# Seven block products instead of eight in the first product of a feed-forward block, after clustered attention, in float32

## The chip, the cores and the metric

One core of one Trainium2 chip runs the whole program. The metric is the device time in microseconds (us); the figure of a kernel is the median of several runs. The core has five engines that run side by side, each with its own queue in program order: TensorE multiplies matrices into PSUM (2 KB banks per partition, eight of them), VectorE and ScalarE do elementwise work and can read PSUM, GpSimd does elementwise work on SBUF, and SyncE here only issues transfers. In the profile they are called PE (with PEld for its weight loads), DVE, ACT, POOL and SP.

## The reference

```python
# q, k, v: (4, 8, 768, 64); centroids: (8, 16, 64)
q_assign = argmax(q_n . c_n); k_assign = argmax(k_n . c_n)      # nearest of 16 centroids
mask   = q_assign[:, :, :, None] == k_assign[:, :, None, :]
scores = where(mask, q @ k.T / sqrt(64), -1e9)
attn   = softmax(scores)                                        # denominator + 1e-9
x      = (attn @ v) -> (4 * 768, 8 * 64) = (3072, 512)
# second block: w_in (512, 2048), w_out (2048, 512)
h = x @ w_in
g = h * (1.0 / (1.0 + exp(-1.702 * h)))
out = (g @ w_out).astype(float32)
```

The weights arrive in float64 and are turned into float32 on the chip. A query attends only to keys whose nearest centroid is its own.

## The kernel before

The program walks through 192 units of attention (two heads, 384 queries, 128 keys each), two units in each of 96 turns `t`. A pair of heads is a tile of 128 partitions; four pairs make one batch, and each pair is visited twice, for the first and the second half of its 768 queries. As soon as the four pairs of one half of one batch are normalised, there are four tiles `xT` of 128 features x 384 tokens, and the second block for these 384 tokens is put into a queue `ffn` of 28 steps. The turns that follow take steps from that queue between their attention work. There are 8 such halves. While half `n` is in attention, half `n-1` is in the second block; the last half runs alone at the end.

```python
pairs = ctx.enter_context(tc.tile_pool(name="pairs", bufs=NPB))      # NPB = HP + 1 = 5
wp = ctx.enter_context(tc.tile_pool(name="wp", bufs=3))
gp = ctx.enter_context(tc.tile_pool(name="gp", bufs=NF))             # NF = 16
yp = ctx.enter_context(tc.tile_pool(name="yp", bufs=2))
ps_s = ctx.enter_context(tc.tile_pool(name="ps_s", bufs=2, space=PS))  # two banks each
ps_o = ctx.enter_context(tc.tile_pool(name="ps_o", bufs=1, space=PS))
ps_m = ctx.enter_context(tc.tile_pool(name="ps_m", bufs=3, space=PS))

def bank():                                   # one of three banks, for all but scores and values
    return ps_m.tile([P, 512], FP32, name="m")
# ... (cut)
def first(f):                                 # 128 of the 2048 columns of x @ w_in, transposed
    round_to((f * P // WN + 1) * NCH)
    ps = bank()
    for c in range(NCH):                      # 4 chunks of the 512 features
        nc.tensor.matmul(out=ps[:, 0:HALF], lhsT=w_in[:, c, f * P:(f + 1) * P],
                         rhs=xT[c], start=(c == 0), stop=(c == NCH - 1))
    g = hs[f] = gp.tile([P, HALF], FP32, name="g")
    nc.scalar.activation(out=g, in_=ps[:, 0:HALF], func=AF.Tanh, scale=0.851)
    nc.vector.scalar_tensor_tensor(out=g, in0=g, scalar=1.0, in1=ps[:, 0:HALF],
                                   op0=ALU.add, op1=ALU.mult)

def second(n, part):                          # 4 of 16 chunks of g @ w_out, for 128 tokens
    # ... (cut)
    for f in range(4 * part, 4 * part + 4):
        nc.tensor.matmul(out=ps[:, 0:DM], lhsT=hs[f][:, n * P:(n + 1) * P],
                         rhs=w_out[:, f, :], start=(f == 0), stop=(f == NF - 1))
    if part == NF // 4 - 1:
        y = yp.tile([P, DM], FP32, name="y")
        nc.scalar.mul(y, ps[:, 0:DM], 0.5)
        nc.sync.dma_start(...)

return ([lambda f=f: first(f) for f in range(NF)]
        + [lambda n=n, part=part: second(n, part) for n in range(NH) for part in range(NF // 4)])
```

The order of one turn, shortened:

```python
for t in range(NT + 2):
    # scores of two units (PE), exps (ACT), mask (DVE; for the later batches) and running sums (POOL)
    # values of the two units of the turn before (PE)
    owed = owed + rate if ffn else 0.0        # rate = 28 / 11.5 steps in a turn
    # every third turn: normalise(g): ones x sums (PE), reciprocal 128x384 and product (DVE)
    # prep of a later pair: transposes, nearest centroid (PE, ACT, DVE)
    while owed >= 1 and ffn:
        ffn.popleft()()
        owed -= 1
```

Each fp32 matmul of the program is carried out as two records in the trace, each with a weight load of its own: the 512 matmuls of `first` are 1024 records.

Of the kernel before, what the change touches and what calls it, by code (L numbers as in the profile page):

```python
# [38 lines left out]
def fast(  # L39
# [33 lines left out]
    NF = DF // P  # L73
# [3 lines left out]
    assert D == 64 and NC == 16 and H * NC == P and NJ == 6 and DM == H * D  # L77

    PS = bass.MemoryType.PSUM
    NPB = HP + 1  # L80
    const = ctx.enter_context(tc.tile_pool(name="const", bufs=1))
    inp = ctx.enter_context(tc.tile_pool(name="inp", bufs=3))
    pairs = ctx.enter_context(tc.tile_pool(name="pairs", bufs=NPB))
    wp = ctx.enter_context(tc.tile_pool(name="wp", bufs=3))
# [1 line left out]
    tmp = ctx.enter_context(tc.tile_pool(name="tmp", bufs=3))  # L86
    ap = ctx.enter_context(tc.tile_pool(name="ap", bufs=4))
    xp = ctx.enter_context(tc.tile_pool(name="xp", bufs=HP + 2))
    gp = ctx.enter_context(tc.tile_pool(name="gp", bufs=NF))
    yp = ctx.enter_context(tc.tile_pool(name="yp", bufs=2))  # L90
    dram = ctx.enter_context(tc.tile_pool(
        name="dram", bufs=2, space=bass.MemoryType.DRAM))
    ps_s = ctx.enter_context(tc.tile_pool(name="ps_s", bufs=2, space=PS))
# [124 lines left out]
    hot = const.tile([P, NJ * 4, 32], BF16, name="hot")  # L218
# [12 lines left out]
                            op0=ALU.add)  # L231
# [22 lines left out]
    T, code, qcode, sT, hots = {}, {}, {}, {}, {}  # L254
# [179 lines left out]
    def values(u):  # L434
        g, kt = divmod(u, NJ)
        p, h = split(g)
        if kt == 0:
            o_of[g] = ps_o.tile([P, 512], FP32, name="o")
        A = A_of.pop(u)
        for a in range(2):  # L440
            nc.tensor.matmul(out=o_of[g][a * D:(a + 1) * D, 0:HALF],  # L441
                             lhsT=v_in[p][:, a, kt, :], rhs=A[:, a, :],
                             start=(kt == 0), stop=(kt == NJ - 1))
# [30 lines left out]

    ffn = deque()

    def ffn_chunks(bh):
        b, h = divmod(bh, 2)
        xT = [xT_of.pop(bh * HP + c) for c in range(NCH)]
        hs, ys = {}, {}  # L480

        def first(f):

            round_to((f * P // WN + 1) * NCH)
            ps = bank()
            for c in range(NCH):
                nc.tensor.matmul(out=ps[:, 0:HALF],  # L487
                                 lhsT=w_in[:, c, f * P:(f + 1) * P],
                                 rhs=xT[c], start=(c == 0),
                                 stop=(c == NCH - 1))  # L490
            g = hs[f] = gp.tile([P, HALF], FP32, name="g")
            nc.scalar.activation(out=g, in_=ps[:, 0:HALF], func=AF.Tanh,  # L492
                                 scale=0.851)
            nc.vector.scalar_tensor_tensor(out=g, in0=g, scalar=1.0,  # L494
                                           in1=ps[:, 0:HALF], op0=ALU.add,
                                           op1=ALU.mult)

        def second(n, part):
            round_to(NW // 2 + 4 * (part + 1))
            if part == 0:  # L500
                ys[n] = bank()
            ps = ys[n]
            for f in range(4 * part, 4 * part + 4):
                nc.tensor.matmul(out=ps[:, 0:DM],  # L504
                                 lhsT=hs[f][:, n * P:(n + 1) * P],
                                 rhs=w_out[:, f, :],
                                 start=(f == 0), stop=(f == NF - 1))
            if part == NF // 4 - 1:
                y = yp.tile([P, DM], FP32, name="y")
                nc.scalar.mul(y, ps[:, 0:DM], 0.5)  # L510
                nc.sync.dma_start(
                    out=out[b * S:(b + 1) * S, :].rearrange(
                        "(p j) n -> p j n", j=NJ)[:, h * NH + n, :], in_=y)

        return ([lambda f=f: first(f) for f in range(NF)]
                + [lambda n=n, part=part: second(n, part)
                   for n in range(NH) for part in range(NF // 4)])

# [5 lines left out]
    TB = 2 * HP * TG  # L524

    prep_at = {}
    for p in range(1, NPAIR):
        b, hp = divmod(p, HP)
        for i in range(2 if p == 1 else 0, len(PREP)):
            if p == 1:  # L530
                t = (i - 2) // 2
            elif b == 0:
                t = (hp - 2) * TG + 1 + i // 2
            else:
                t = b * TB + (-20, -8, -2, 1)[hp] + i
            prep_at.setdefault(t, []).append((p, i))
    loads = deque((p, w) for p in range(NPAIR) for w in range(2))
    for _ in range(3):
# [6 lines left out]
        if i in (1, 3) and loads:  # L545
            load_qk(*loads.popleft())

    rate = (NF + NH * (NF // 4)) / (TB / 2 - 0.5)
    owed = 0.0
# [4 lines left out]
    for t in range(NT + 2):  # L554
        us = range(2 * t, 2 * t + 2) if t < NT else ()
        for u in us:
            scores(u)
        if t == 0:
            prep(0, 6)
        for u in us:  # L560
            part(u)
        for u in us:
            exps(u)
        second = t >= TB // 2
        if second:
# [24 lines left out]
        if second and t % 2:  # L590
            round_next()


    ok = const.tile([P, 2, 2 * NPAIR], FP32, name="ok")
# [4 lines left out]
    for _ in range(NF // 2):  # L599
        ffn.popleft()()  # L600
# [5 lines left out]
    nc.vector.tensor_scalar(out=bad, in0=okt, scalar1=-1.0, scalar2=1.0,  # L606
                            op0=ALU.mult, op1=ALU.add)
    while ffn:
        ffn.popleft()()
# [443 lines left out]
```

## Time and profile before

| | |
|---|---|
| median of 3 runs | 1087.48 us (1084.81 to 1087.8) |
| profiled execution, first to last instruction | 1087.3 us |
| granted TensorE clock, mean | 0.990 of full speed |
| PE busy | 1049.0 us (96%), 3982 records |
| DVE busy | 490.8 us (45%) |
| ACT busy | 354.8 us (33%) |
| POOL busy | 296.9 us (27%) |

A row of the list of groups gives the source line, engine and operation, what it writes and reads, partitions x elements, how many there are, then busy time and mean duration of one in ns, and after the second bar the idle time of that engine just before them with what ended most of it. Busy time is the time that is covered: two overlapping matmul records are counted once, so that busy time divided by count is less than the mean duration. In the row of 40 slices a digit is the busy share of a slice in tenths.

### The profile page before, as it was taken

The page shows a single profiled execution, that of the slowest core. Times are in us where ns is not written, and L with a number is a line of the kernel's source. Part 1 is how long each engine was busy: PE and PEld are TensorE (multiplying, and loading weights), DVE is VectorE, ACT ScalarE, POOL GpSimd, SP SyncE. Part 2 cuts the span into 40 slices and gives each one's busy share as a digit, 9 for nine tenths or more (in the row PEclk, how much of TensorE's full clock was granted, in tenths as well). Part 3 has the DMA queues.
Part 4 walks back from the last instruction along what each step waited for, and adds up shares of the span by engine and source line. Part 5 has one row for each costly group of instructions (what it writes and reads, how often), then busy time and mean ns, then how long its engine had stood idle before and what let it go on. Part 6 is the DMA issues. An engine that isn't in the chain of part 4 may idle for free. (4 is left out here: it accounts for less than half of the span.)

```text
span 1087.3 us, 10456 instructions
## 1 busy us (share of the span) xinstructions
PE 1049.0 (96%) x3982; PEld 492.6 (45%) x3982; DVE 490.8 (45%) x744; ACT 354.8 (33%) x665; POOL 296.9 (27%) x168
## 2 busy tenths in 40 slices
PE   7878799999999999999999999999999999999997
PEld 3423344445544455444454445444554445444543
DVE  3889999225442344424453164423552344431200
ACT  3755555223422333223432233223332133311100
POOL 2644223213232333123231142222332333230000
PEclk9998899999999999999999999999999999999999
DMA  7623443110100010002100000010000000000000
GB/s 199 165 81 116 131 133 111 46 49 17 49 23 27 10 30 15 31 25 54 51 23 17 15 20 15 15 48 32 8 7 12 10 10 1 1 10 20 1 11 22
DMA packets 64813, 45.13 MB, mean 42 GB/s; under 512 B 51953, under 2 KB 57585, under 8 KB 64753
## 3 DMA queue, kind: packets, MB, share of 16 engines
q1 hardware_dynamic: 64608, 44.33, 14.3%
q8 instruction: 33, 0.54, 0.2%
q14 instruction: 28, 0.22, 0.1%
q10 hardware_dynamic: 144, 0.03, 0.0%
HBM read 38.04 MB, written 6.31 MB: 41 GB/s over the span
## 5 line engine op out<-in xcount | busy, mean ns | idle before, releaser
L430 POOL TENSOR_TENSOR sum<-sum,A 128x768 f32<-128x768 f32 x128 | 235.5, 1840 | 461.3 <-DVE A L420 364.1
L487 PE MATMUL m<-x,w_in 128*128 128x384 f32 x1024 | 347.1, 494 | 9.7 <-ACT T L267 4.4
L504 PE MATMUL m<-w_out,g 128*128 128x512 f32 x768 | 337.8, 594 | 0.7 <-ACT short L282 0.7
L420 DVE SCALAR_TENSOR_TENSOR A<-qb,code,s 128x384 f32<-128x384 uint8 x288 | 157.6, 609 | 274.6 <-ACT s L409 251.9
L487 PEld LDWEIGHTS m<-x,w_in 128*128 128x128 f32 x1024 | 192.2, 192 | 149.1 <-issue 16.3
L504 PEld LDWEIGHTS m<-w_out,g 128*128 128x128 f32 x768 | 143.3, 190 | 175.6 <-issue 171.5
L494 DVE SCALAR_TENSOR_TENSOR g<-g,m 128x384 f32<-128x384 f32 x128 | 70.0, 553 | 220.4 <-ACT g L492 220.3
L384 PE MATMUL s<-T,T 64*128 64x384 f32 x768 | 152.9, 517 | 9.7 <-ACT A L409 9.6
L409 ACT ACTIVATE s<-s 128x768 f32<-128x768 f32 x144 | 107.9, 792 | 136.0 <-PE s L384 136.0
L441 PE MATMUL o<-A,inv 128*64 128x384 f32 x768 | 146.3, 502 | 0.0
L492 ACT ACTIVATE g<-m 128x384 f32<-128x384 f32 x128 | 61.7, 487 | 196.4 <-PE m L487 196.3
L430 POOL TENSOR_TENSOR sum<-A 128x768 f32<-128x768 f32 x32 | 60.0, 1876 | 215.6 <-DVE A L420 179.5
L384 PEld LDWEIGHTS s<-T,T 64*128 64x128 f32 x768 | 66.6, 189 | 94.6 <-issue 52.2
L456 DVE RECIPROCAL short<-m 128x384 f32<-128x384 f32 x32 | 81.6, 2551 | 25.8 <-PE m L453 25.8
L441 PEld LDWEIGHTS o<-A,inv 128*64 128x64 f32 x768 | 46.8, 137 | 84.8 <-issue 84.1
L510 ACT ACTIVATE y<-m 128x512 f32<-128x512 f32 x24 | 14.3, 595 | 155.8 <-PE m L504 142.7
L468 ACT ACTIVATE short<-short 128x384 f32<-128x384 f32 x32 | 16.7, 523 | 111.2 <-DVE x L458 111.2
L409 ACT ACTIVATE A<-s 128x768 f32<-128x768 f32 x48 | 36.1, 804 | 22.0 <-PE s L398 22.0
L267 ACT COPY T<-m 128x384 f32<-128x384 f32 x64 | 29.7, 480 | 37.2 <-PE m L262 37.1
L262 PE MATMUL m<-ident,in 128*128 128x128 f32 x192 | 33.9, 298 | 3.1 <-ACT T L267 1.7
L163 ACT ACTIVATE e<-e,low 128x512 int32<-128x512 int32 x32 | 23.1, 722 | 28.8 <-DVE e L159 28.8
L262 PEld LDWEIGHTS m<-ident,in 128*128 128x128 f32 x192 | 21.5, 146 | 22.4 <-issue 11.9
(68 smaller groups left out, 373.5 us busy)
## 6 DMA issues: line engine op xcount, KB each, us to landing
raw<-in_moe_w_in_dram SPq DMA_DIRECT2D x16, 512.0 KB
raw<-in_moe_w_out_dram SPq DMA_DIRECT2D x16, 512.0 KB
in<-in_q_dram SPq DMA_DIRECT2D x32, 192.0 KB
in<-in_k_dram SPq DMA_DIRECT2D x32, 192.0 KB
inv<-in_v_dram SPq DMA_DIRECT2D x16, 384.0 KB
out_dram<-y SPq DMA_DIRECT2D x24, 256.0 KB
qb<-line SPq DMA_DIRECT2D x12, 192.0 KB
line<-row SPq DMA_DIRECT2D x12, 1.5 KB
```

What stands on the lines that cost most here:

```text
L262: nc.tensor.transpose(out=ps[:, n * P:(n + 1) * P], in_=qk_in[p, w][:, h * NH + n].rearrange("p a d -> p (a d)"), identity=ident)
L267: nc.scalar.copy(dst, ps[:, 0:HALF])
L384: nc.tensor.matmul(out=ps[:, a, 0:HALF], lhsT=T[p, 1][rows, kt * P:(kt + 1) * P], rhs=T[p, 0][rows, h * HALF:(h + 1) * HALF], start=True, ...
L409: nc.scalar.activation(out=A_of[u] if p < HP else s, in_=s, func=AF.Exp, scale=SCALE)
L420: nc.vector.scalar_tensor_tensor(out=A_of[u][:, a, :], in0=qcode[p][:, a, h * HALF:(h + 1) * HALF], scalar=code[p][:, kt % NH, 1, kt // NH ...
L430: nc.gpsimd.tensor_tensor(out=sum_of[g], in0=A_of[u - 1] if kt == 1 else sum_of[g], in1=A, op=ALU.add)
L441: nc.tensor.matmul(out=o_of[g][a * D:(a + 1) * D, 0:HALF], lhsT=v_in[p][:, a, kt, :], rhs=A[:, a, :], start=(kt == 0), stop=(kt == NJ - 1))
L456: nc.vector.reciprocal(out=rec, in_=ps[:, 0:HALF])
L487: nc.tensor.matmul(out=ps[:, 0:HALF], lhsT=w_in[:, c, f * P:(f + 1) * P], rhs=xT[c], start=(c == 0), stop=(c == NCH - 1))
L492: nc.scalar.activation(out=g, in_=ps[:, 0:HALF], func=AF.Tanh, scale=0.851)
L494: nc.vector.scalar_tensor_tensor(out=g, in0=g, scalar=1.0, in1=ps[:, 0:HALF], op0=ALU.add, op1=ALU.mult)
L504: nc.tensor.matmul(out=ps[:, 0:DM], lhsT=hs[f][:, n * P:(n + 1) * P], rhs=w_out[:, f, :], start=(f == 0), stop=(f == NF - 1))
```

## The change

Write the product of 256 rows of `w_in`-columns, 512 features and 384 tokens as a 2x2x2 product of blocks: the weights' output columns f and f + 8 (row blocks 0 and 1), the features 0..255 and 256..511 (inner blocks), and the tokens 0..191 and 192..383. Eight block products are needed in the plain way. With sums and differences of blocks taken beforehand and others taken afterwards, seven are enough (the scheme of Strassen in Winograd's form). The sums over the weights are taken once; those over `x` once for each half; those over the results for every pair of column blocks. The purpose is to give TensorE one product in eight less.

The first of the eight halves keeps the plain form. In each of the other seven, two column blocks (f = 7 and f = 15) stay plain and the other fourteen go by pairs through `seven`. A tile of `x` is partly overwritten by its sums, after the two plain blocks have used it. Space for the sums of weights comes from the buffers of the weight conversion and from one buffer less in the pool `pairs` (four pairs are held instead of five, and a pair of the next batch is prepared later) and in the pool `yp`.

```diff
-    NPB = HP + 1
+    NPB = HP
+    TOK = HALF // 2
+    FB = NF // 2
-    gp = ctx.enter_context(tc.tile_pool(name="gp", bufs=NF))
-    yp = ctx.enter_context(tc.tile_pool(name="yp", bufs=2))
+    gp = ctx.enter_context(tc.tile_pool(name="gp", bufs=FB))
+    yp = ctx.enter_context(tc.tile_pool(name="yp", bufs=1))
+    fp = ctx.enter_context(tc.tile_pool(name="fp", bufs=1))
 ...
+    def sums_w(c, step):            # on VectorE, 896 columns, in turns 22 and 23
 ...  (four sums for each of two feature chunks)
+    def gelu(g, h, on_gpsimd=False):
+        nc.scalar.activation(out=g, in_=h, func=AF.Tanh, scale=0.851)
+        if on_gpsimd:
+            nc.scalar.activation(out=g, in_=g, func=AF.Copy, bias=1.0)
+            nc.gpsimd.tensor_tensor(out=g, in0=g, in1=h, op=ALU.mult)
+        else:
+            nc.vector.scalar_tensor_tensor(out=g, in0=g, scalar=1.0, in1=h,
+                                           op0=ALU.add, op1=ALU.mult)
 ...
+        def sums_x():
+            for c in range(2):
+                for i, a, b in ((3, B(1, 1, c), B(0, 1, c)),
+                                (1, B(0, 1, c), B(0, 0, c)),
+                                (2, B(1, 1, c), T(1, c)),
+                                (4, B(1, 0, c), T(2, c))):
+                    nc.vector.tensor_tensor(out=T(i, c), in0=a, in1=b, op=ALU.subtract)
+
+        def seven(f):
 ...  (product: two matmuls, 128x128 weights, 192 columns; pair: two products into one bank)
+            q = fp.tile([P, 2, TOK], FP32, name="q", bufs=2)
+            p16 = pair((A(0, 0), X(0, 0)), (S(2), Tx(2)))
+            nc.scalar.copy(q[:, 0], p16[:, 0])
+            add(q[:, 1], p16[:, 1], q[:, 0])
+            p57 = pair((S(1), Tx(1)), (A(1, 0), Tx(3)))
+            add(V, p57, q[:, 1:2, :].broadcast_to((P, 2, TOK)))
+            add(q[:, 1], p57[:, 1], V[:, 0])
+            p34 = pair((S(4), X(1, 1)), (A(1, 1), Tx(4)))
+            add(V, p34, V)
+            p2 = bank()[:, 0:TOK]
+            product(p2, A(0, 1), X(1, 0))
+            add(q[:, 0], p2, q[:, 0])
+            half_g(f)
+            g = gs[f].rearrange("p i (j n) -> p (i j) n", j=2)
+            gelu(g[:, 0:4:3, :], q)
+            gelu(g[:, 1:3, :], V, on_gpsimd=True)
 ...
-        return ([lambda f=f: first(f) for f in range(NF)]
-                + [lambda n=n, part=part: second(n, part)
-                   for n in range(NH) for part in range(NF // 4)])
+        if bh == 0:
+            steps = [(1.0, lambda f=f: first(f)) for f in range(NF)]
+        else:
+            steps = [(1.0, lambda f=f: first(f)) for f in (FB - 1, NF - 1)]
+            steps += [(0.0, sums_x)]
+            steps += [(1.75, lambda f=f: seven(f)) for f in range(FB - 1)]
+        return steps + [(4 / 3, lambda n=n, part=part: second(n, part))
+                        for n in range(NH) for part in range(NF // 4)]
 ...
-                t = b * TB + (-20, -8, -2, 1)[hp] + i
+                t = b * TB + (-8, -5, -2, 1)[hp] + i
 ...
+        if not ffn:
+            rate = 0.0
+        elif not rate:
+            rate = sum(w for w, f in ffn) / (TB / 2 - 0.5)
 ...
-        while owed >= 1 and ffn:
-            ffn.popleft()()
-            owed -= 1
+        while ffn and owed >= ffn[0][0] / 2:
+            w, f = ffn.popleft()
+            f()
+            owed -= w
```

`V` is one tile for the whole program (the place of `hot`, which is no longer needed by then); `q` has two buffers.

More of the change, by code (lines that the diff above doesn't have):

```diff
@@ L79, in fast @@
     PS = bass.MemoryType.PSUM
-    NPB = HP + 1
+    NPB = HP
+    TOK = HALF // 2
+    FB = NF // 2
+    WB = (FB - 1) * P
     const = ctx.enter_context(tc.tile_pool(name="const", bufs=1))
@@ L475, in fast, with block, S_at @@
     ffn = deque()
+    Ts, S_of = {}, {}
+    def block(row, col, c, lo=0, hi=WB):
+        at = row * FB * P
+        return w_in[:, 2 * col + c, at + lo:at + hi]
+    def S_at(i, c, lo, hi):
+        if c and lo >= WB - P:
+            return Ts[i][:, HALF:HALF + P]
+        return S_of[i, c][:, lo:hi]
+    def sums_w(c, step):
+        if c == step == 0:
+            for i in (1, 2, 4):
+                Ts[i] = wp.tile([P, WN], FP32, name="T", tag="e")
+                S_of[i, 0] = wp.tile([P, WN, 2], I32, name="raw").bitcast(
+                    FP32).rearrange("p n t -> p (n t)")[:, 0:WB]
+                S_of[i, 1] = fp.tile([P, WB - P], FP32, name=f"S{i}")
+        for r in ((0, WB - P), (WB - P, WB)) if c else ((0, WB),):
+            out, a, b, op = (
+                (S_at(1, c, *r), block(1, 0, c, *r), block(1, 1, c, *r),
+                 ALU.add),
+                (S_at(2, c, *r), S_at(1, c, *r), block(0, 0, c, *r),
+                 ALU.subtract),
+                (S_at(4, c, *r), block(0, 1, c, *r), S_at(2, c, *r),
+                 ALU.subtract),
+                (block(1, 0, c, *r), block(0, 0, c, *r), block(1, 0, c, *r),
+                 ALU.subtract),
+            )[step]
+            nc.vector.tensor_tensor(out=out, in0=a, in1=b, op=op)
+    def gelu(g, h, on_gpsimd=False):
[6 more added lines that the diff above has]
+                                           op0=ALU.add, op1=ALU.mult)
     def ffn_chunks(bh):
@@ L479, in ffn_chunks, with half_g @@
         xT = [xT_of.pop(bh * HP + c) for c in range(NCH)]
-        hs, ys = {}, {}
+        gs, ys = {}, {}
+        def half_g(f):
+            if f % FB not in gs:
+                gs[f % FB] = gp.tile([P, 2, HALF], FP32, name="g")
+            return gs[f % FB][:, f // FB, :]
         def first(f):
@@ L490, in first, with B @@
                                  stop=(c == NCH - 1))
[L491 to L496, printed above, removed]
+            gelu(half_g(f), ps[:, 0:HALF])
+        def B(row, col, c):
+            return xT[2 * row + c][:, col * TOK:(col + 1) * TOK]
@@ new lines, in T @@
+        def T(i, c):
+            return (B(0, 1, c) if i == 1 else
+                    Ts[{2: 1, 3: 2, 4: 4}[i]][:, c * TOK:(c + 1) * TOK])
+        def sums_x():
[4 more added lines that the diff above has]
+                                (4, B(1, 0, c), T(2, c))):
+                    nc.vector.tensor_tensor(out=T(i, c), in0=a, in1=b,
+                                            op=ALU.subtract)
@@ new lines, in seven, with product, S, A @@
+        def seven(f):
+            cols = (f * P, (f + 1) * P)
+            def product(out, A, x):
+                for c in range(2):
+                    nc.tensor.matmul(out=out, lhsT=A(c), rhs=x(c),
+                                     start=(c == 0), stop=(c == 1))
+            def S(i):
+                return lambda c: S_at(i, c, *cols)
+            def A(i, j):
+                return lambda c: block(i, j, c, *cols)
+            def X(i, j):
+                return lambda c: B(i, j, c)
+            def Tx(i):
+                return lambda c: T(i, c)
+            def pair(one, other):
+                ps = bank()
+                product(ps[:, 0:TOK], *one)
+                product(ps[:, TOK:HALF], *other)
+                return ps[:, 0:HALF].rearrange("p (i n) -> p i n", i=2)
+            def add(out, a, b):
+                nc.vector.tensor_tensor(out=out, in0=a, in1=b, op=ALU.add)
+            q = fp.tile([P, 2, TOK], FP32, name="q", bufs=2)
[14 more added lines that the diff above has]
+            gelu(g[:, 1:3, :], V, on_gpsimd=True)
@@ L504, in second @@
                 nc.tensor.matmul(out=ps[:, 0:DM],
-                                 lhsT=hs[f][:, n * P:(n + 1) * P],
+                                 lhsT=half_g(f)[:, n * P:(n + 1) * P],
                                  rhs=w_out[:, f, :],
@@ L513, in second @@
                         "(p j) n -> p j n", j=NJ)[:, h * NH + n, :], in_=y)
[L515 to L517 removed]
+        if bh == 0:
[6 more added lines that the diff above has]
+                        for n in range(NH) for part in range(NF // 4)]
+    V = hot.rearrange("p n c -> p (n c)").bitcast(FP32).rearrange(
+        "p (i n) -> p i n", i=2)
     NT = NU // 2
@@ L546, in prep @@
             load_qk(*loads.popleft())
-    rate = (NF + NH * (NF // 4)) / (TB / 2 - 0.5)
-    owed = 0.0
+    owed = rate = 0.0
+    sums_at = {TB - 2 + c: [(c, step) for step in range(4)] for c in range(2)}
     for p, i in [(0, i) for i in range(6)] + [(1, i) for i in range(2)]:
@@ L586, in fast @@
             round_next()
-        while owed >= 1 and ffn:
-            ffn.popleft()()
-            owed -= 1
+        while ffn and owed >= ffn[0][0] / 2:
+            w, f = ffn.popleft()
+            f()
+            owed -= w
         if second and t % 2:
             round_next()
-    ok = const.tile([P, 2, 2 * NPAIR], FP32, name="ok")
+        if t in sums_at:
+            for c, step in sums_at[t]:
+                sums_w(c, step)
+    ok = short()[:, 0:4 * NPAIR].rearrange("p (i g) -> p i g", i=2)
     nc.vector.tensor_scalar(out=ok, in0=sums, scalar1=LIMIT, scalar2=None,
@@ L598, in fast @@
     nc.vector.tensor_reduce(out=ok1, in_=ok, axis=AX.XY, op=ALU.min)
-    for _ in range(NF // 2):
-        ffn.popleft()()
+    for _ in range(NF // 4):
+        ffn.popleft()[1]()
     ps = bank()
@@ L608, in fast @@
     while ffn:
-        ffn.popleft()()
+        ffn.popleft()[1]()
         if len(ffn) == 4:
```

## The prediction

> **What bounds the kernel now.** I read the page's first two parts, then busy time by stretches, then the groups, then the last stage in order of time. First the page's totals and slices:
>
> ```profile
> PE 1049.0 (96%) x3982; PEld 492.6 (45%) x3982; DVE 490.8 (45%) x744; ACT 354.8 (33%) x665; POOL 296.9 (27%) x168
> ...
> PE   7878799999999999999999999999999999999997
> PEld 3423344445544455444454445444554445444543
> DVE  3889999225442344424453164423552344431200
> ```
>
> PE is full from the sixth slice on; DVE is full only in the slices before the eighth, while the weights are converted. Stretches (us, then busy us with count for PE, PEld, DVE, ACT, POOL, then clock, DMA share, GB/s):
>
> ```profile
> 0.00:190.00 190.00, 160.67 (x789) 74.05 (x790) 157.56 (x233) 103.98 (x191) 72.56 (x44) 0.95 0.47 134
> 190.00:998.00 808.00, 804.95 (x2968) 375.99 (x2967) 323.71 (x492) 240.53 (x455) 224.29 (x124) 1.00 0.08 23
> 998.00:1040.00 42.00, 42.00 (x131) 24.52 (x130) 8.97 (x19) 7.96 (x16) 0.00 (x0) 1.00 0.02 7
> ```
>
> From 190 us on PE idles 3 us in 808: any matmul time removed there comes off the end, and any wait put in PE's way is added in full. DVE has 40% there, so it is free on average. The groups that the change touches, or whose durations I need:
>
> ```profile
> L430 POOL TENSOR_TENSOR sum<-sum,A 128x768 f32<-128x768 f32 x128 | 235.5, 1840 | 461.3 <-DVE A L420 364.1
> L487 PE MATMUL m<-x,w_in 128*128 128x384 f32 x1024 | 347.1, 494 | 9.7 <-ACT T L267 4.4
> ...
> L494 DVE SCALAR_TENSOR_TENSOR g<-g,m 128x384 f32<-128x384 f32 x128 | 70.0, 553 | 220.4 <-ACT g L492 220.3
> ...
> L441 PEld LDWEIGHTS o<-A,inv 128*64 128x64 f32 x768 | 46.8, 137 | 84.8 <-issue 84.1
> L456 DVE RECIPROCAL short<-m 128x384 f32<-128x384 f32 x32 | 81.6, 2551 | 25.8 <-PE m L453 25.8
> ```
>
> The first block waits for practically nothing (9.7 us in 347). The last stage in order of time (start, us):
>
> ```profile
> 1021.98 18.23 PE L487 MATMUL m<-x,w_in 128*128 128x384 f32 x56
> 1040.04 41.36 PE L504 MATMUL m<-w_out,g 128*128 128x512 f32 x96
> ```
>
> A record of 384 columns lasts 486 ns, so 56 of them are (18.23 - 0.486) / 55 = 322.6 ns apart; 96 records of 512 columns (594 ns each) are (41.36 - 0.594) / 95 = 429 ns apart. The slope is 106.5 / 128 = 0.832 ns a column, and 322.6 = 384 x 0.832 + 3. So 192 columns should follow each other every 162.5 ns, **if the weight load does not bind**. A load of 128 columns lasts 190 ns, more than 162.5. But a load of 64 columns lasts 137: 0.83 ns a column, so 128 columns occupy the path for 106 ns and some 84 ns are latency. The transposes show that the latency overlaps:
>
> ```profile
> L262 PEld LDWEIGHTS m<-ident,in x192: 137/141/231, 5.4 to 781.8; 128*128 128x128 f32 x192
> L262 PE MATMUL m<-ident,in x192: 272/273/447, 5.4 to 781.9; 128*128 128x128 f32 x192
> ...
> 544.34 0.49 PE L262 MATMUL m<-ident,in 128*128 128x128 f32 x3
> ```
>
> Three in 0.49 us are (0.49 - 0.273) / 2 = 109 ns apart, while each has a load of 141 ns before it.
>
> **What the Trainium skill says.** "TensorE: Matmul & The Clock Gate", section "LDWEIGHTS (loading the stationary operand)", puts the load at columns / 1.2 ns, 107 ns for 128: the slope above agrees. The same page, "Part 2: What happens when you issue a matmul", says that the next load is pulled ahead under the running matmul; the 322.6 ns agree. "SBUF — State Buffer", section "Who interferes with whom", says that a VectorE instruction with two SBUF inputs contends with a GpSimd instruction that reads SBUF: here the 128x384 product of two SBUF tiles (L458) has a mean of 695 ns and a minimum of 558. No page bears on a chain of additions out of three PSUM banks.
>
> **The change, part by part.** *Removed from PE.* One `seven` replaces two `first`: 16 records x 322.5 = 5.16 us become 28 records x 162.5 = 4.55 us, a gain of 0.61 us and not an eighth of everything, because the scheme saves 2 of 16 halves and each record pays its 2.5 ns more often. There are 7 halves x 7 = 49: **-29.9 us**, all in the stretch where PE is full.
>
> *Added to DVE, ACT, POOL.* From 553 ns for 384 columns and 220 to 226 ns for 64 (small groups of the list by form) DVE costs 1.02 ns a column plus 160, so 192 columns take 0.36. A `seven` has three adds of 192 and two of 384 and one fused step of 384: about 2.75 us against 1.1 before. ACT: a copy of 192 (0.33, from 487 for 384 and 595 for 512), two tanh and a copy of 384: 1.8 us against 1.0. POOL: half of 1840, 0.92 us, for 49. Averages stay far from full: about 49 x 1.65 = 81 us more on DVE in 808, some 50%.
>
> *The chain inside one `seven`*, from PE's start, engines free: p16 ends 1.5; copy 1.9; add 2.3; p57 ends 2.8; add to V 3.4; add 3.8; p34 ends 4.1; add 4.65; p2 ends 4.7; add 5.1; tanh of q 5.6; tanh of V 6.1; copy 6.6; POOL 7.6. V is one tile and is written again at 2.8 of the next one, that is 7.35: 0.3 us late, in DVE's queue. p57's bank is then free about 0.5 us before it is wanted. So a run of sevens is bound by PE, barely: any 0.5 us that DVE or ACT spends on other work first shows on PE.
>
> *Waits that this makes.* (a) `sums_x` is 8 dependent DVE steps of 192 columns. The second product needs the seventh: 7 x 0.36 = 2.5 us, after the fused step of f = 15 (about 1.3 us behind PE). Against it PE has only 0.65 us of work until c = 0 and little more: about 3 us of waiting where a `seven` directly follows. By the new rate (30.25 / 11.5 = 2.63 a turn, or 32 / 11.5 after the first half) that is so in the odd halves and at the end, and in the even ones a turn's attention lies between: 4 x 3 = **+12 us**. (b) In a turn with normalise (2.55 + 0.7 us on DVE ahead of the adds) or with an assignment of clusters (about 2.9 us on DVE) three banks don't last: 0.5 to 1 us, some two or three such turns in each of six halves: **+8 us**, a choice between 4 and 14. (c) The run of sevens at the end: +0.5 us. (d) Preparing pair 4 later takes some 3 us of DVE out of the full stretch before 190 us and puts as much PE into the full one after; sums of weights (8 steps on 896 columns, about 10 us of DVE in turns 22 and 23, when DVE is mostly idle): 0 to +1 us. One y buffer: y's are 13.8 us apart at the closest (16 x 0.43 x 2), no wait.
>
> Sum: 1087.5 - 29.9 + 12 + 8 + 0.5 + 0.5 = 1078.6; as (a) and (b) are guesses on the careful side, I take **1076 us**.
>
> **Rivals.** *The load binds* and 28 records go at 190: 5.32 us a `seven`, +8 us instead of -30, total about 1110. For it: the recorded 190 ns. Against it: the transposes. I give it 1 in 12. *The waits are hidden*: DVE is half idle, the two plain blocks and attention give slack, and nearly all of 30 us arrives: 1060. For it: PE's work between dependent steps is long, and steps are spread over turns. Against: the chain's 0.5 us of slack. 1 in 6. *DVE becomes the bound* in the turns with two sevens: masks 2.2, sevens 5.5, and 3 more in some: 11 of about 12.5 us, with contention from POOL's running sums perhaps all. Then waits double to 40 us and the time is the old one, 1087 to 1095. 1 in 6.
>
> **Range and chances.** Low 1062 is a gain of 30 with 5 lost; high 1092 is the DVE rival. The limits of 2% are 1065.7 and 1109.2: faster 0.18, within 0.77, slower 0.05.
>
> **What would show it.** Records of 128x192 at 162.5 ns apart and 329 ns long say step one is right; 190 apart says the load binds. PE busy near 1020. Idle of PE before the `seven` matmuls put down to DVE's difference of x (about 12 us in 4 places) proves (a); idle put down to DVE's adds, clustered at reciprocals and assignments, proves (b). Idle put down to POOL's product would mean that V, not the banks, is what I undervalued. I am wrong if the whole of PE's idle after 190 us is below 8 us or above 40.

## The result and the profile after

The changed kernel takes **1117.46 us** (median of 4 runs, 1115.0 to 1119.18) against 1087.64 us for the kernel before: a ratio of **1.0277, with a 95% interval of 1.0247 to 1.0307**. The change makes the program 2.8% slower. The prediction was 1076 us with a range of 1062 to 1092.

The page of the changed kernel, first two parts:

```profile
PE 1038.5 (93%) x4570; PEld 571.4 (51%) x4570; DVE 603.0 (54%) x1008; ACT 388.5 (35%) x763; POOL 346.1 (31%) x217
...
PE   7878898998999999998999999999899999999997
PEld 4323453446744476444664467444674447644863
DVE  3889998445643565425763276434565256532520
```

PE now falls below nine tenths in some slices of the stretch where it was full, and DVE has risen, but is far from full in every slice after the eighth. By stretches (columns as in the prediction):

```profile
0.00:190.00 190.00, 163.80 (x785) 75.86 (x785) 159.14 (x228) 103.04 (x188) 72.98 (x44) 0.94 0.46 131
190.00:998.00 808.00, 767.31 (x3396) 431.16 (x3397) 413.44 (x718) 265.17 (x530) 260.97 (x164) 0.99 0.08 23
```

From 190 to 998 us PE idles 808 - 767.3 = 40.7 us, against 3 before. The groups of the seven products (L575), listed by form:

```profile
L575 PE MATMUL m<-T,w_in 128*128 128x192 f32 x392 | 81.8, 332 | 0.0
L575 PE MATMUL m<-x,w_in 128*128 128x192 f32 x392 | 81.6, 335 | 15.2 <-DVE q L597 14.5 <-ACT T L271 0.5
L575 PE MATMUL m<-x,raw 128*128 128x192 f32 x196 | 49.8, 336 | 6.2 <-DVE short L460 5.9
```

And what PE waited for, in total, times and the longest (L597 are the sums over results, L567 the sums over x, L460 the reciprocal in normalise):

```profile
PE m L575 <- DVE q L597: 14.5, 18, 1.2
PE m L575 <- DVE T L567: 13.0, 11, 1.6
PE s L388 <- ACT A L413: 9.0, 4, 3.2
PE m L575 <- DVE short L460: 5.9, 7, 1.2
```

This view understates what is lost. When PE stops, the record before is still draining, and the drain counts as busy: a record of 192 columns lasts 326 ns while the next may follow after 162. So I added up, from the starts and ends of the records, by how much the distance of the ends of two successive records exceeds 162.5 ns. Inside the 49 runs of `seven` this is 49 us: 16.4 before the second product (its weights are sums, its moving operand is a sum of x), 9.5 before the third pair (p34), 17.7 before p2, the rest before the next p16 and in two stretches at half TensorE clock. Of the losses before p34 and p2, 21.0 us lie in the nine turns with normalise, 2.3 us in each, and 5.9 us in the six turns with an assignment of clusters. The matmuls themselves run as reckoned: of 1340 distances between the starts of successive records of 192 columns, 1192 lie between 160 and 165 ns.

One turn shows most of it. Timeline of the changed kernel (start, length in us; L601 is ScalarE's copy out of p16, L472 and L474 the check of the reciprocals):

```profile
543.38 0.81 PE L457 MATMUL m<-sum,ones 128*64 128x384 f32 x4
...
544.69 0.92 PE L575 MATMUL m<-x,w_in 128*128 128x192 f32 x4
...
545.60 2.55 DVE L460 RECIPROCAL short<-m 128x384 f32<-128x384 f32 x1
...
548.18 0.70 DVE L462 TENSOR_TENSOR x<-x,short 128x384 f32<-128x384 f32 x1
548.20 0.59 PE L575 MATMUL m<-x,raw 128*128 128x192 f32 x2 [0.65 <-DVE short L460]
...
548.91 0.52 ACT L472 ACTIVATE short<-short 128x384 f32<-128x384 f32 x1 [3.58 <-DVE x L462]
...
549.56 0.61 ACT L474 ACTIVATE short<-short,top 128x384 f32<-128x384 f32 x1
...
550.17 0.30 ACT L601 COPY q<-m 128x192 f32<-128x192 f32 x1
550.50 0.36 DVE L597 TENSOR_TENSOR q<-m,q 128x192 f32<-128x192 f32 x1 [1.63 <-ACT q L601]
550.92 0.92 PE L575 MATMUL m<-x,w_in 128*128 128x192 f32 x4 [1.15 <-DVE q L597]
```

p16 was ready at about 546.3. Its copy on ScalarE runs at 550.17, because ahead of it in ScalarE's queue stands the check, which waits for the reciprocal and the product of x on DVE. Only then is p16's bank read to the end, and only then may p2 be written. The third pair had waited before that (548.20) for the bank that the reciprocal reads. Two queues and three banks, and PE, which needs neither result, stands still for 0.9 and then 1.4 us.

### The profile page after: what moved, and what is told of

Same layout as the page of the kernel before. It is cut to its first block, busy times and chain, and to the rows that moved or that the text cites. A ratio compares the mean times of both kernels' runs of the same rounds, so it can differ in the third digit from the quotient of the medians.

```text
span 1114.3 us, 12189 instructions
## 1 busy us (share of the span) xinstructions
PE 1038.5 (93%) x4570; PEld 571.4 (51%) x4570; DVE 603.0 (54%) x1008; ACT 388.5 (35%) x763; POOL 346.1 (31%) x217
## 5 line engine op out<-in xcount | busy, mean ns | idle before, releaser
L622 PE MATMUL m<-w_out,g 128*128 128x512 f32 x768 | 342.5, 598 | 4.9 <-DVE w_out L181 3.8
L388 PE MATMUL s<-T,T 64*128 64x384 f32 x768 | 155.4, 524 | 9.1 <-ACT A L413 9.0
L528 POOL TENSOR_TENSOR g<-g,hot 128x384 f32<-128x384 f32 x49 | 48.9, 997 | 238.5 <-ACT g L527 238.5
L460 DVE RECIPROCAL short<-m 128x384 f32<-128x384 f32 x32 | 81.6, 2551 | 30.0 <-PE m L457 30.0
L575 PE MATMUL m<-x,w_in 128*128 128x192 f32 x392 | 81.6, 335 | 15.2 <-DVE q L597 14.5
L547 PE MATMUL m<-x,w_in 128*128 128x384 f32 x240 | 82.7, 496 | 8.0 <-DVE g L530 5.4
L525 ACT ACTIVATE g<-q 128x384 f32<-128x384 f32 x49 | 25.6, 523 | 163.0 <-DVE q L597 163.0
L575 PE MATMUL m<-T,w_in 128*128 128x192 f32 x392 | 81.8, 332 | 0.0
L575 PEld LDWEIGHTS m<-x,w_in 128*128 128x128 f32 x392 | 63.6, 190 | 29.4 <-DVE q L597 18.1
L575 PEld LDWEIGHTS m<-T,w_in 128*128 128x128 f32 x392 | 68.5, 195 | 0.0
L547 PEld LDWEIGHTS m<-x,w_in 128*128 128x128 f32 x240 | 45.2, 193 | 42.4 <-DVE g L530 6.3
L472 ACT ACTIVATE short<-short 128x384 f32<-128x384 f32 x32 | 16.7, 523 | 121.4 <-DVE x L462 121.4
L575 PE MATMUL m<-x,raw 128*128 128x192 f32 x196 | 49.8, 336 | 6.2 <-DVE short L460 5.9
```

The source lines that it names most:

```text
L388: nc.tensor.matmul(out=ps[:, a, 0:HALF], lhsT=T[p, 1][rows, kt * P:(kt + 1) * P], rhs=T[p, 0][rows, h * HALF:(h + 1) * HALF], start=True, ...
L460: nc.vector.reciprocal(out=rec, in_=ps[:, 0:HALF])
L472: nc.scalar.activation(out=rec, in_=rec, func=AF.Copy, accum_out=sums[:, 0, g:g + 1])
L525: nc.scalar.activation(out=g, in_=h, func=AF.Tanh, scale=0.851)
L528: nc.gpsimd.tensor_tensor(out=g, in0=g, in1=h, op=ALU.mult)
L575: nc.tensor.matmul(out=out, lhsT=A(c), rhs=x(c), start=(c == 0), stop=(c == 1))
```

## The experiments

All ratios are to the kernel before, run beside it on the same chip. "Against before" is the difference of the medians. The last column is read from the one profiled execution of each kernel, from the first matmul of scores in turn 24 to the end; the kernel before takes 868.0 us there. It is worth having because, up to turn 24, the TensorE clock is at half for some 17 to 41 us, at other places in each execution. The kernel with the freed bank shows this, as it was profiled twice: its turn 12 begins at 81.8 us in one execution and 82.9 in the other, and from turn 24 on both take 854.6 us.

| kernel | us | against before | ratio (95%) | from turn 24, us |
|---|---|---|---|---|
| changed kernel | 1117.46 | +29.8 | 1.0277 (1.0247 to 1.0307) | 890.2 |
| check late | 1103.84 | +15.3 | 1.0135 (1.0108 to 1.0162) | 875.9 |
| normalise and check late | 1103.62 | +15.1 | 1.0126 (1.0105 to 1.0146) | 875.9 |
| sums of x first | 1098.09 | +9.6 | 1.0081 (1.0061 to 1.0101) | 870.9 |
| all plain | 1096.42 | +7.9 | 1.0059 (1.0040 to 1.0079) | 868.1 |
| all plain, old rule | 1097.17 | +9.5 | 1.0081 (1.0065 to 1.0098) | 871.5 |
| all plain, five pairs | 1089.68 | +2.0 | 1.0014 (1.0007 to 1.0020) | 864.6 |
| check late + sums of x first | 1085.31 | -2.4 | 0.9969 (0.9957 to 0.9981) | 858.4 |
| the same + bank freed by ScalarE | 1081.75 | -5.9 | 0.9933 (0.9912 to 0.9954) | 854.6 |
| the same again, another chip | 1082.31 | -5.1 | 0.9962 (0.9944 to 0.9980) | 854.6 |
| the same + both halves of p16 copied | 1092.68 | +4.1 | 1.0037 (1.0024 to 1.0050) | 862.5 |
| products only (sums over results left out) | 1075.16 | -13.4 | 0.9872 (0.9846 to 0.9899) | 846.6 |
| bank freed, reciprocal over 64 columns | 1065.67 | -21.8 | 0.9790 (0.9775 to 0.9805) | 844.6 |

My theory after the trace was: the order in the queues of ScalarE and VectorE, together with three banks, stops PE; the rival: VectorE is simply full in these turns, and moving one wait only makes another.

**Check late.** In the turn loop of the changed kernel:

```diff
-        if recs:
-            check(*recs)
         if second or t and t % 4 != 3:
             round_next()
         while ffn and owed >= ffn[0][0] / 2:
             ...
+        if recs:
+            check(*recs)
```

> Only the two ScalarE steps of the check of reciprocals move, from before the second block's steps of a turn to after them. Theory A (ScalarE's queue): in turns with normalise the check waits for the reciprocal and the product of x on VectorE, the copy out of p16 waits behind it, p16's bank stays taken and the matmuls of p2 lose 1.42 us; nine such turns, so about 1104 to 1106 us (12 us less than the changed kernel's 1117.5), and the waits of 1.4 us before p2 go. Theory B (VectorE itself is full in these turns): the adds are behind the reciprocal anyway, and the time stays within 3 us of 1117.

Measured: 1103.84 us, 14.5 us less against before. What PE waits for in this run:

```profile
PE m L575 <- DVE T L567: 13.0, 11, 1.6
PE m L575 <- DVE short L460: 6.0, 7, 1.2
PE m L575 <- DVE q L597: 4.4, 10, 0.6
```

The wait for the adds fell from 14.5 to 4.4 us, the longest from 1.2 to 0.6. By the distances of records the waits before p2 went from 17.7 us in 15 places to 4.95 in 6. No wait before p2 is left in the nine turns with normalise, and p34 and p2 together lose 0.9 us in each of them instead of 2.3. Two ScalarE steps that nothing in the block needs were worth nearly half of the slowdown: ScalarE's queue is shown.

**Normalise late.** As above, and `normalise(g)` too is moved behind the steps, except for the last of a half, whose x the next steps need.

```diff
-        if g is not None and second:
+        late = g is not None and second and g % HP != HP - 1
+        if g is not None and second and not late:
             normalise(g)
         ...  (the steps of the turn)
+        if late:
+            normalise(g)
         if recs:
             check(*recs)
```

> Normalise (where it is not the last of a half) and the check both move behind the second block's steps of the turn. Theory A (order in the queues of VectorE and ScalarE, three banks): the waits before p34 (0.2 to 1.5 us) and before p2 (1.42 us) go in all nine turns, some 21 us, so about 1096 us. Theory B (VectorE full): the work of VectorE is the same and only moves by half a turn, so the waits turn up before masks or scores instead; 1110 us or more.

Measured: 1103.62 us, the same as with the check alone. The waits left the turns with normalise and appeared in the turns after them: 0.8 to 1.4 us before p34 or 1.7 before p2, and 0.49 before the next p16. The reciprocal then stands at the head of VectorE's queue one turn later. So for the reciprocal, unlike the check, the rival holds: 3.25 us of VectorE have to stand before somebody's adds.

**Sums of x first.** T2 is written as T3 + B00, so that only T1 overwrites x:

```diff
 ...  (sums_x in two parts: T3, T2, T4 for True, T1 for False)
-            steps = [(1.0, lambda f=f: first(f)) for f in (FB - 1, NF - 1)]
-            steps += [(0.0, sums_x)]
+            steps = [(0.0, lambda: sums_x(True))]
+            steps += [(1.0, lambda f=f: first(f)) for f in (FB - 1, NF - 1)]
+            steps += [(0.0, lambda: sums_x(False))]
```

> Of the eight sums over x the six that need not overwrite x (T3, T2 = T3 + B00, T4) are taken before the two plain column blocks, the two of T1 in place after them. Theory A: the waits of 1.9 and 1.2 us (or 0.13 and 1.2) before the second product in each of seven halves, 16.4 us in all, shrink to about 0.5 us each, and the two stretches at half TensorE clock that follow such waits (1.7 us each) go: about 1101 us. Rival: VectorE's late start is from the fused step of the plain blocks and the sums' place makes no difference: within 3 us of 1117.

Measured: 1098.09 us, 20.2 us less against before. No wait for the sums of x is left before the second product. Instead, in four halves, the pair p57, whose first product uses T1, waits 0.4 to 0.5 us. The gain is more than the 16.4 us of waits. In the changed kernel two of these waits were followed by a stretch at half clock:

```profile
200.00:258.00 58.00, 53.60 (x221) 24.32 (x218) 27.92 (x43) 17.70 (x35) 16.27 (x9) 1.00 0.21 57
258.00:262.00 4.00, 4.00 (x16) 4.00 (x15) 1.27 (x3) 0.10 (x1) 0.00 (x0) 0.57 0.00 0
262.00:300.00 38.00, 35.52 (x211) 27.27 (x210) 25.55 (x48) 16.08 (x35) 14.04 (x10) 1.00 0.08 17
```

The granted clock is 0.57 between 258 and 262 us, and records of 192 columns are 320 ns apart there instead of 162. The rival, that the place of the sums doesn't matter, is out.

In the changed kernel the three even halves among the seven lose 1.3 us before the second product, although a turn's attention lies between there. The first of the eight sums of x takes 1.7 us in each of these three halves and 0.35 in the other four. It starts under a running sum of GpSimd and ends 0.2 us after it, so that all sums behind it are some 1.35 us later:

```profile
382.58 3.71 POOL L434 TENSOR_TENSOR sum<-sum,A 128x768 f32<-128x768 f32 x2 [3.88 <-DVE A L424]
384.79 1.70 DVE L567 TENSOR_TENSOR T<-x 128x192 f32<-128x192 f32 x1
```

That is read from the trace; no run takes the running sum away.

**All plain, and its two halves.** First everything of the change but the seven products and the sums of weights:

```diff
-        if bh == 0:
+        if True:
-    sums_at = {TB - 2 + c: [(c, step) for step in range(4)] for c in range(2)}
+    sums_at = {}
```

> All eight halves in the plain form, no sums of weights; everything else of the change stays (four pairs held, later preparation, one y buffer, the new rule for taking steps). Theory A: what is beside the seven products costs the 5 us by which the first quarter (before any seven products) became longer, and no more: 1090 to 1095 us. Rival: the later preparation and the new rule cost in every quarter, 4 x 5: 1105 us or more.

Measured: 1096.42 us, +7.9. The expectation had 1090 to 1095. By the first matmul of scores in turn 24 the kernel before is at 219.3 us and this one at 226.7: nearly all of the loss is there. Then the rule was set back, with the buffers and the preparation as changed:

```diff
-        if not ffn:
-            rate = 0.0
-        elif not rate:
-            rate = sum(w for w, f in ffn) / (TB / 2 - 0.5)
+        rate = (NF + NH * (NF // 4)) / (TB / 2 - 0.5)
 ...
-        while ffn and owed >= ffn[0][0] / 2:
-            w, f = ffn.popleft()
-            f()
-            owed -= w
+        while ffn and owed >= 1:
+            w, f = ffn.popleft()
+            f()
+            owed -= 1
```

> All plain, with the buffers and the late preparation of the change but with the rule for steps of before. The all-plain run lost about 8 us, all in the first quarter. Theory A (late preparation): pair 4 is now prepared while VectorE still converts weights for the steps in the queue, so the loss stays: 1094 to 1097 us. Theory B (rule): in the first half the new rule takes 2.78 plain blocks a turn instead of 2.43 and runs into weights that are not yet converted, so the loss goes: 1087 to 1090 us.

and the buffers and the preparation, with the new rule:

```diff
-    NPB = HP
+    NPB = HP + 1
-                t = b * TB + (-8, -5, -2, 1)[hp] + i
+                t = b * TB + (-20, -8, -2, 1)[hp] + i
-    yp = ctx.enter_context(tc.tile_pool(name="yp", bufs=1))
+    yp = ctx.enter_context(tc.tile_pool(name="yp", bufs=2))
```

> All plain, with the new rule for steps but five pairs held, the early preparation and two y buffers as before. Theory A (late preparation): the loss goes, 1087 to 1090 us. Theory B (rule): the loss stays, 1094 to 1097 us. Both a part: about 1092 us in both this run and its counterpart.

Measured: +9.5 us with the old rule, +2.0 us with the old buffers and preparation. So holding four pairs and preparing later costs 9.5 us under the old rule and 5.9 (7.9 less 2.0) under the new one; the two parts do not simply add. The new rule has a wait of its own: it makes PE wait 3.4 us (five pairs) or 3.9 us (all plain) for weights that are not yet converted, and none with the old rule. Pair 4 used to be prepared in turns 4 to 10, when PE had room; but these turns did not become shorter without it (turn 12 begins at 82.1 us before and 81.8 in the run with the old rule), and turns 16 to 22 became longer. The half clock does not explain it: it costs "sums of x first", which in these turns does the same as all plain, 0.7 us up to turn 12 and the run with five pairs 0.9, and they begin turn 12 at 79.9 and 80.3 us. With the old rule the starts of turns 24, 48, 72 and 95 are later than before by 3.2, 4.5, 5.8 and 6.7 us: a part in the first quarter, and about 1.2 us in each later one. The single y buffer was not tried by itself; in the changed kernel a store of y lands in 2.0 us and they are 13.7 us or more apart, so it should have no part in it.

**Both waits away.** The check late and the sums of x first together.

> The seven-product kernel with the check after the steps of the turn and the six sums of x before the plain blocks. If the two waits are independent, the gains add: 1117.5 - 13.6 - 19.4 = 1084.5 us. If VectorE or ScalarE is full in these turns, the second gain is partly eaten: 1090 us or more.

Measured: 1085.31 us, 32.2 us less against before, where the two gains added make 34.7. They are nearly independent. What remains:

```profile
PE m L575 <- DVE short L460: 5.5, 7, 1.1
PE m L575 <- DVE q L597: 4.4, 10, 0.6
```

**The bank of the sums freed.** On top of the last:

```diff
-        nc.vector.reciprocal(out=rec, in_=ps[:, 0:HALF])
+        nc.scalar.copy(rec, ps[:, 0:HALF])
+        nc.vector.reciprocal(out=rec, in_=rec)
```

> As the run with both, and the sums of a half are copied out of their bank by ScalarE (about 0.48 us) so that the bank is free before VectorE gets to the reciprocal. Theory A (three banks): the waits before p34 in turns with normalise (0.8 to 1.5 us in most of nine) go, 7 to 9 us: about 1076 us. Theory B (VectorE's queue): p34's matmuls start, but p2 and the next p16 then wait for the adds behind the reciprocal, and at most 3 us are gained.

Measured: 1081.75 us, 3.6 us less against before, and 3.8 us less from turn 24 on. The wait for the reciprocal's bank is gone, and most of it has turned into waits for the adds:

```profile
PE m L576 <- DVE q L598: 8.1, 19, 0.8
```

By the distances of records the waits before p34 went from 8.8 to 1.4 us and those before p2 rose from 5.0 to 11.3. That is theory B of the expectation, with a gain a little over its limit of 3 us. This is the fastest kernel here that computes the whole; it was run once more.

> The same kernel as the run with the freed bank, on the same chip as the run beside it: the ratio to the kernel before should again be 0.993, so that it is faster than both kernels by a known amount.

Measured: 1082.31 us, a ratio of 0.9962 (0.9944 to 0.9980), a little short of the 0.993 expected; the two intervals overlap at 0.995. It beats both kernels, the one before by four to seven parts in a thousand. By medians alone the gain of the freed bank would be in doubt, as "check late + sums of x first" has 0.9969 on another chip; it rests on the last column, 858.4 against 854.6 us twice.

**Both halves of p16 copied.**

```diff
-            nc.scalar.copy(q[:, 0], p16[:, 0])
-            add(q[:, 1], p16[:, 1], q[:, 0])
+            nc.scalar.copy(q, p16)
+            add(q[:, 1], q[:, 1], q[:, 0])
```

> As the run with the freed bank, and ScalarE copies both halves of p16 instead of the first, so that p16's bank no longer waits for VectorE; the add is then taken from SBUF. Theory A (the bank of p16 is what p2 waits for): the waits before p2, 11.3 us in 18 places, go: 1081.75 - 11 = about 1071 us. Theory B (VectorE's queue behind reciprocal or assignment is long enough to hold p57's bank too): about half comes back before the next p16, 1076 us. Theory C (VectorE is full there, every freed bank only moves the wait): 1080 us or more.

Measured: 1092.68 us: not the 10 us of gain hoped for, but 10 us of loss. p2 waits no longer (0.4 us in all), and the next p16 waits 15.2 us for p57's bank. The list of groups by form shows a slower add, first in this run, then in the one before it:

```profile
L598 DVE TENSOR_TENSOR q<-q 128x192 f32<-128x192 f32 x49 | 31.9, 652 | 14.4 <-ACT q L602 14.4
```

```profile
L598 DVE TENSOR_TENSOR q<-m,q 128x192 f32<-128x192 f32 x98 | 34.4, 352 | 12.0 <-ACT q L602 10.7
```

The mean of 652 ns hides two kinds. Of the 49 adds with both inputs in SBUF, the 24 that start while a GpSimd instruction runs take 885 to 1211 ns, and each ends 0.21 to 0.22 us after that instruction; the other 25 take 342 to 359 ns. In the run before, with one input in PSUM, 30 adds start under a GpSimd instruction and take 348 to 359 ns. In the last stage, where no attention runs:

```profile
1026.63 1.00 POOL L529 TENSOR_TENSOR g<-g,hot 128x384 f32<-128x384 f32 x1 [4.01 <-ACT g L528]
1026.95 0.89 DVE L598 TENSOR_TENSOR q<-q 128x192 f32<-128x192 f32 x1 [0.78 <-ACT q L602]
```

This agrees with the Trainium skill, "SBUF — State Buffer", section "Who interferes with whom", by which a VectorE instruction with two SBUF inputs contends with a GpSimd instruction that reads SBUF; I had cited the section for the product of x in normalise and did not apply it to this edit. From turn 24 on the edit costs 7.9 us: 3.0 more by distances inside `seven`, and 3.7 more in waits before the second block. Of these waits the first line is from this run and the second from the one before it:

```profile
PE m L623 <- DVE q L598: 5.1, 4, 2.1
PE m L623 <- DVE q L598: 1.4, 4, 0.6
```

That the slow adds make these waits is argued from the trace, not tried by a run. The other 3.6 us of the loss lie before turn 24, where nothing of this edit runs; the mean clock was 0.91 there against 0.93, which may be the reason.

**Products only.** From the run with the sums of x first; the sums over results are left out, the output is thus not the product:

```diff
-            (all copies, adds and the two gelu of `seven`)
+            p16 = pair((A(0, 0), X(0, 0)), (S(2), Tx(2)))
+            gelu(g[:, 0:2, :], p16)
+            p57 = pair((S(1), Tx(1)), (A(1, 0), Tx(3)))
+            gelu(g[:, 2:4, :], p57)
+            p34 = pair((S(4), X(1, 1)), (A(1, 1), Tx(4)))
+            p2 = bank()[:, 0:TOK]
+            product(p2, A(0, 1), X(1, 0))
```

> The seven products alone: all sums over results are left out, and of the four banks the first two are turned into g as plain ones are, so its output isn't the product; sums over x as in the run that takes six of them first. It measures the first term of the prediction by itself. Theory A (records of 192 columns at 162.5 ns): the all-plain run less 29.9 us, plus about 2 for the sums of x in place: 1067 to 1069 us. Theory B (weight loads or anything else in TensorE eats it): 1085 us or more.

Measured: 1075.16 us, which is 21.3 us less than all plain, against before. By distances 7.7 us of waits are left in `seven` even so (0.1 to 0.5 us before p2, 15 times, and less before p34 and p57), which makes up most of the 8.6 us to the 29.9. The first term is confirmed, and even with no sums over results three banks for four groups cost something.

**Short reciprocal.** From the run with the freed bank; the reciprocal is left out for 320 of 384 columns, so the output is another one:

```diff
-        nc.vector.reciprocal(out=rec, in_=rec)
+        nc.vector.reciprocal(out=rec[:, 0:64], in_=rec[:, 0:64])
```

> As the run with the freed bank, but the reciprocal is taken over 64 of its 384 columns (the rest of the sums goes through as it is, so the output is another one): some 0.5 us of VectorE instead of 2.55, 32 times. Theory A (the adds stand behind the reciprocal in VectorE's queue): the waits before p2 in the turns with normalise, about 6 us, go, those in the turns with an assignment of clusters (0.5 to 0.9 us, 7 us in all) stay: 1081.75 - 6 = 1076 us, a little less where x is awaited. Theory B (ScalarE or PSUM banks hold p2 there): within 2 us of 1081.75.

Measured: 1065.67 us, 16.6 us less than the kernel with the freed bank beside it (1082.31). The waits before p2 fell from 11.3 to 4.9 us and none is left in a turn with normalise, while those of 0.8 to 0.9 us in the turns with an assignment stayed: so far as expected. Inside `seven` this is 8.2 us by distances, and from turn 24 to the end it is 10.0 us. Another 4.4 us lie before turn 24, where VectorE converts weights and was nearly full, but where the mean clock was also 0.96 against 0.94; the two are not separated. VectorE's queue, not the banks alone, holds p2 in these turns.

## Why the prediction was wrong

The signs of the terms were right and their sizes were not. The prediction's own sum was 1078.6 us; the measured time is 39 us above it, and half of that is term (b).

- **Records of 192 columns every 162.5 ns, the load not binding: right**, by 1192 of 1340 distances. The rival to which I gave 1 in 12 is out. **-29.9 us: right**, as the run with products only shows (21.3 us gained, 7.7 of waits left).
- **The chain inside one `seven` "is bound by PE, barely": right** where it was reckoned, with the engines free. In the last stage of the run with the freed bank one `seven` begins 4.55 us after another, and DVE waits 0.5 us for GpSimd's product each time without PE losing anything. V was not the problem: no wait of PE for GpSimd is found.
- **(a), sums of x, "4 x 3 = +12 us": too small.** The four places cost 3.1 us each, as said. That attention "lies between" in the even halves was so, and still these three places lost 1.3 us each: the first of the eight sums stood behind GpSimd and took 1.35 us more than elsewhere. This is the contention that the prediction names for the product of x and does not apply to the sums. In all it was 16.4 us in waits; putting the sums first brought 20.2 us, half clock included.
- **(b), normalise and assignment, "+8 us, a choice between 4 and 14": the step that failed.** It was 27.2 us, p34 and p2 together. In the six turns with an assignment the two lost 1.0 us a turn, inside the forecast of 0.5 to 1; in the nine with normalise they lost 2.3. I counted the work that VectorE has ahead of the adds and left out that ScalarE has the check ahead of its copy out of p16, and that the check itself waits for that work of VectorE. So the chain p16, copy, add was not delayed by 3.25 us but by 3.25 and 1.2 more, and the copy that could have run early ran last. 14.5 us hung on it, shown by moving the check: the turns with normalise then lose 0.9 us each, inside the forecast too. So the picture of three banks that don't last was right, and the queue of ScalarE was missing from it. The "guess on the careful side" was thus on the other side, and I even took 2.6 us off for it.
- **(d), late preparation, "0 to +1 us": wrong**, 5.9 us under the new rule and 9.5 under the old one. I argued that DVE work removed from the early stretch pays for PE work added to the full one. The early turns did not get shorter: that exchange was assumed, not read from a view.
- Of the rivals, *the load binds* came nearest in time (1110 us), by luck: the distances rule out its mechanism. *VectorE becomes the bound* named too short a time (1087 to 1095 us), but its "waits double to 40 us" was near in size (49) and partly right in cause: the reciprocal and the assignment are waits of VectorE's queue, the check is one of ScalarE's, and the sums of x are a matter of place and of contention with GpSimd.
- The signs to look for: "PE busy near 1020" was a poor one, since PE's drain after each wait counts as busy (1038.5). "Idle of PE after 190 us above 40" came true at once: 40.7 us up to 998 alone.

The account, against before: late preparation and rule +7.9, products -29.9, waits and half clock in `seven` +49, together +27 of the measured 29.8. Where the last 2.8 us lie was not followed up.

What stays open: why the early turns don't shorten when pair 4's preparation leaves them, and how much of the differences before turn 24, in the runs that copy both halves and shorten the reciprocal, is the clock's.

## What to carry to other kernels

When an operation's result must be read by several engines before its bank is free, list for each of these engines what stands ahead in its queue, and what that in turn waits for; a ScalarE step that nobody needs soon, placed ahead of a copy that frees a bank, cost 14.5 us here and moving it took two lines. Fewer matmul columns with the same banks mean more hand-overs for each us of matmul, so in a kernel where TensorE is full, the saving is real (21 us without the sums) but as large as the waits that it makes. Space that is taken from buffers held ahead has a price of its own (6 to 9.5 us here), best measured alone with the new arithmetic left out.

## What the runs showed of the hardware that I had not expected

- A VectorE addition with both inputs in SBUF did not share with GpSimd but stood behind it. All 24 adds of 192 columns that started under a GpSimd instruction ended 0.21 to 0.22 us after it did, after 0.89 to 1.21 us; the other 25 took 0.34 to 0.36 us, six of them started 0.2 us before a GpSimd instruction. With one input in PSUM the same add took 0.35 to 0.36 us, 30 times under a GpSimd instruction. So taking an operand out of PSUM early, to free a bank, made the add slower wherever GpSimd was at work.
- Waits of 1.9 and 1.2 us, with two matmul records between them, were enough in two of four such places for a stretch of 3.4 us at half TensorE clock, with 320 ns between records of 192 columns. The Trainium skill, "TensorE: Matmul & The Clock Gate", section "What's actually happening", gives a window of about 3.4 us without work, free-running, after which the clock is halved; both waits together, 3.1 us, are shorter than that. Why two of the four places were hit and two not, no run here shows.
- A weight load that is recorded with 190 ns stands under a matmul every 162 ns without any loss.
